# A decode layer's last microseconds on one core: output copies that no longer wait for each other, residual products issued ahead of the last matrix, and weight loads in fewer pieces

## The chip, the core and the metric

The kernel runs on one core of a Trainium2 chip. The metric is the device time of one execution in microseconds (us). The median of three runs of the kernel before is 190.62 us (190.58 to 190.89).

## What is computed

One token goes through attention with a cache of 16384 keys and values, then through a mixer and an MLP. The reference, cut to its core:

```python
def _A_ref(x, k_cache, v_cache, wq, wo):        # 32 query heads, 8 key heads, 128 wide
    q = (x @ wq) ...                            # one token, D = 512
    scores = einsum("bhqd,bhkd->bhqk", q, k) * (Dh ** -0.5)
    o = einsum("bhqk,bhkd->bhqd", softmax(scores), v)
    return o... @ wo
def _B_ref(x, w1, w2, w3, w4):
    h = _gelu(_layernorm(x) @ w1)
    hs = (four quarters of h, shifted along the sequence, zeros shifted in) @ w2
    x1 = x + hs
    return x1 + _gelu(_layernorm(x1) @ w3) @ w4   # F = 1792

h = x + _A_ref(_layernorm(x), ...)
return h + _B_ref(_layernorm(h), ...)
```

The sequence has length 1, so each shifted quarter holds only the zeros that were shifted in: hs is 0, x1 is x, and w1 and w2 are not needed.

## The kernel before, in words

Each engine has its own list of operations, written by hand in program order. A small class (`Program`, from L25) derives the waits: an operation names the tiles that it reads (`r`) and writes (`w`), and the PSUM banks that it touches (`bank`). Two engines that name the same bank wait for each other in program order, even if neither writes it. A list is issued in order, so an operation that waits holds everything behind it on its engine.

**Attention.** Four pairs of key heads are worked off one after another. Keys come in halves of 4 MB into `kb[0]` and `kb[1]`, values in 8 MB into `vb` (for the last pair in two pieces of 4 MB). DVE transposes the keys into `kt` (L583), PE multiplies them with the query (L600), ACT takes the exponentials (L621), and PE multiplies these with the values (L636). DVE gathers the pair's rows out of PSUM (L652 to L660) into `o_m`.

**Weights at the end.** The key buffers are used again: `wo` lies over `kb[0]`, `w3` and `w4` over `kb[1]`. All loads are issued on SP's queue by `load` (L434) in program order. `wo` is cut by `WO` (L329) into heads, `w3` by `W3` (L331) into chunks of 128 rows, and `w4` by `W4` (L332) into chunks m; each piece has a key of its own, `("r", 0, n)` for wo and `("r", 1, n)` for w3 and then w4. Each piece holds a stretch of every partition's row, so a piece of 12 heads moves 128 runs of 12 KB. SP waits until DVE has transposed the last keys of a buffer before it issues the loads that overwrite it.

**The tail.** DVE sums `o_m` into `o_f` (L696) and casts it to `o_b` (L698). PE multiplies it with wo: 32 matmuls, one for each head, in four column groups of 32 that run side by side (L702). DVE copies the result (L706), PE sums it over rows (L708), and `row_sums` (L479 to L495) makes the residual sum `hr`, its transpose `hT` and the moments of the layernorm. ACT adds the mean's negative into `hc` (L714), and PE multiplies `hc` with w3: 16 matmuls, four chunks by four column groups (L720). Meanwhile `variance` gives the scale, and DVE forms `xsum` (L724, L725), which is the residual plus its layernorm. ACT applies gelu in two halves (L729) and DVE transposes each half into `hcol` (L733). PE then multiplies `hcol` with w4: 14 chunks m by four column groups (L747). Between m = 6 and m = 7 it adds `xsum` by four fp32 products with the identity (L740); an fp32 matmul shows as two passes in the trace. All of it goes into one half of one PSUM bank, `n_ps` (bank "mn"). At the end ACT copies partitions 0 to 63 of it into `fin` (L752), DVE partitions 64 to 127 (L754), and SP sends two rows of `fin` to the output (L755).

Two operations without a function (L736 for DVE, L745 for PE) stand for branches that are never taken (L150, L314). They cut the two engines' last instructions into a block of their own.

Of the kernel before, what the change touches and what calls it, by code (L numbers as in the profile page):

```python
# [325 lines left out]
NCH = D // 128  # L326
FQ = FM // 4
NHC = FM // 128
WO = ((0, 12), (12, 24), (24, 30), (30, 32))  # L329
VP = 2  # L330
W3 = ((0, 2), (2, 3), (3, 4))  # L331
W4 = ((0, 5), (5, 10), (10, 13), (13, 14))  # L332
BLOCK = (0, 2, 1, 3)
PAIRS = HKV // 2
# [8 lines left out]
def bass_sequential_preLN__gqa_block_cached__mixer_s_mlp__decode_kernel(  # L343
# [13 lines left out]
    with ExitStack() as ctx:  # L357
# [18 lines left out]
        ident_f = sb("ident_f", [128, 128], FP32)  # L376
# [28 lines left out]
        o_f = sb("o_f", [128, 32], FP32)  # L405
        o_b = sb("o_b", [128, 32], BF16)
# [5 lines left out]
        xsum = sb("xsum", [128, 128], FP32)  # L412
# [3 lines left out]
        fin = sb("fin", [64, 256], BF16)  # L416
# [13 lines left out]
        m_ps, n_ps = mn_ps[:, 0:256], mn_ps[:, 256:512]  # L430


        def load(name, dst, src, key, by="SP", also=()):
            P.op(by, lambda e: e.dma_start(dst, src), w=[key, *also], dma=name)  # L434
# [24 lines left out]
        def dve(fn, r=(), w=(), bank=()):  # L459
            return P.op("DVE", fn, r, w, bank)  # L460

        def act(fn, r=(), w=(), bank=()):
            return P.op("ACT", fn, r, w, bank)
# [4 lines left out]
        def pe(fn, r=(), w=(), bank=(), also=()):  # L468

            return P.op("PE", fn, r, w, bank, also=also)  # L470

        def piece(cuts, m):
            return [lo <= m < hi for lo, hi in cuts].index(True)

        def copies(col, n):

            return col.to_broadcast([col.shape[0], n])
# [19 lines left out]
        def variance(i):  # L497

            s, S = st[i], ("st", i)

            dve(lambda e: e.scalar_tensor_tensor(s[:, 2:3], s[:, 0:1], s[:, 0:1], s[:, 1:2],
                                                 ALU.mult, ALU.add), r=[(S, 0)], w=[(S, 2)])
            dve(lambda e: e.tensor_scalar(s[:, 3:4], s[:, 2:3], 0.0, -1.0, ALU.min, ALU.mult),
                r=[(S, 2)], w=[(S, 3)])
            for n in range(1 + i):
                mul, add = (1.0 + EPS, EPS * EPS) if n else (1.0, EPS)
                dve(lambda e, n=n, mul=mul, add=add: e.tensor_scalar(s[:, 4 + n:5 + n], s[:, 3:4], mul, add,  # L507
                                                                     ALU.mult, ALU.add), r=[(S, 3)], w=[(S, 4 + n)])
            pool(lambda e: e.tensor_tensor(s[:, 6:7 + i], s[:, 4:5 + i], expo[:, 0:1 + i], ALU.pow),  # L509
                 r=["expo"] + [(S, 4 + n) for n in range(1 + i)], w=[(S, 6 + n) for n in range(1 + i)])  # L510
# [17 lines left out]
            r=["ident", "x4"], w=["quarter"])  # L528
        pe(lambda e: e.matmul(O_ps[0][:, 0:128], quarter[:, :, :].rearrange("p q u -> p (q u)"), x4[:, :],
                              start=True, stop=True), r=["quarter"], w=[("O", 0)], bank=[("O", 0)])  # L530
# [7 lines left out]
            r=["ident_f"], w=["row32"])  # L538
        dve(lambda e: e.tensor_reduce(maskdd[:, :], ident_f[:, :].rearrange("p (n d) -> p d n", d=4), AX.X, ALU.add),
            r=["ident_f"], w=["maskdd"])  # L540
# [6 lines left out]
        for z, m, key, mk in ((zo, rowgh, "zo", "rowgh"), (zd, maskgh, "zd", "maskgh")):  # L547
# [5 lines left out]
            r=["hT", (("st", 0), 0), (("st", 0), 6)] + [("v", x) for x in range(VP)], w=["xn"])  # L553
# [3 lines left out]
        for i, key in enumerate(keys):  # L557
            P.part("query", i)
            for k in range(NCH):
                pe(lambda e, k=k: e.matmul(row[:, bass.ds(P.b, 512)], copies(xn[:, k:k + 1], 128),  # L560
                                           wq_k[:, k, bass.ds(P.c, REP * DH)], start=(k == 0), stop=(k == NCH - 1)),
                   r=["xn"], also=[("v", x) for x in range(VP)], w=["n" if key == "mn" else key], bank=[key])
        P.part()
        for g in range(2):
            half = banks[64 * g:64 * g + 64, PAIRS * g:PAIRS * g + PAIRS, :].rearrange("p j c -> p (j c)")
            for b in range(2):
# [3 lines left out]
                    r=["n" if x == "mn" else x for x in keys[PAIRS * g:PAIRS * g + PAIRS]], w=["qcol"],  # L570
                    bank=keys[PAIRS * g:PAIRS * g + PAIRS])
# [112 lines left out]
        act(lambda e: e.activation(scr[0:1, 1:2], mean4[0:1, 0:1], ACTF.Gelu_apprx_tanh), r=["mean4"], w=["scr"])  # L684
        for n, (lo, hi) in enumerate(WO):
            load(f"wo{n}", wo_sb[:, lo * D:hi * D], A_wo.rearrange("(p r) c -> p (r c)", p=128)[:, lo * D:hi * D],
                 ("r", 0, n))
        w3_in = B_w3.rearrange("(p k) f -> p k f", p=128)
        for n, (lo, hi) in enumerate(W3):
            load(f"w3{n}", w3_sb[:, lo:hi, :], w3_in[:, lo:hi, :], ("r", 1, n))  # L690
        w4_in = B_w4.rearrange("(p m) c -> p m c", p=128)
        for n, (lo, hi) in enumerate(W4):
            load(f"w4{n}", w4_sb[:, lo:hi, :], w4_in[:, lo:hi, :], ("r", 1, len(W3) + n))


        dve(lambda e: e.tensor_reduce(o_f[:, :], o_m[:, :, :].rearrange("p d r -> p r d"), AX.X, ALU.add),  # L696
            r=["o_m"], w=["o_f"])
        dve(lambda e: e.tensor_copy(o_b[:, :], o_f[:, :]), r=["o_f", ("r", 0, 0)], w=["o_b"])  # L698

        for r_ in range(32):  # L700
            q = r_ % 4
            pe(lambda e, r_=r_, q=q: e.matmul(O_ps[0][32 * q:32 * q + 32, :], copies(o_b[:, r_:r_ + 1], 32),  # L702
                                              wo_sb[:, r_ * D:(r_ + 1) * D], start=(r_ < 4), stop=(r_ >= 28)),
               r=["o_b"] + [("r", 0, n) for n in (piece(WO, r_),) if n], w=[("O", 0)], bank=[("O", 0)])
        h_ps, hkey = banks[:, 6, :], "spare0"
        dve(lambda e: e.tensor_copy(osum[:, :], O_ps[0][:, :]), r=[("O", 0)], w=["osum"], bank=[("O", 0)])  # L706
        for q in range(4):
            pe(lambda e, q=q: e.matmul(h_ps[32 * q:32 * q + 32, 0:128], copies(row32[:, 0:1], 32),  # L708
                                       osum[:, q * 128:(q + 1) * 128], start=True, stop=True),
               r=["osum", "row32"], w=[hkey], bank=[hkey])  # L710
# [4 lines left out]
            r=["hT", (S, 0)] + [("r", 1, 0)], w=["hc"])  # L715


        for k in range(NCH):
            for q in range(4):
                pe(lambda e, k=k, q=q: e.matmul(s_ps[32 * q:32 * q + 32, 0, 0:FQ], hc[:, k, :],  # L720
                                                w3_sb[:, k, q * FQ:(q + 1) * FQ], start=(k == 0), stop=(k == NCH - 1)),
                   r=["hc"] + [("r", 1, n) for n in (piece(W3, k),) if n], w=[("s", 0)], bank=[("s", 0)])
        variance(1)
        dve(lambda e: e.tensor_scalar(xs[:, :], hr[:, :], s[:, 0:1], None, ALU.add), r=["hr", (S, 0)], w=["xs"])  # L724
        dve(lambda e: e.scalar_tensor_tensor(xsum[:, :], xs[:, :], s[:, 6:7], hr[:, :], ALU.mult, ALU.add),  # L725
            r=["hr", "xs", (S, 6)], w=["xsum"])
        for n in range(2):
# [6 lines left out]
                hcol[:, lo:hi, :].rearrange("p m u -> p (m u)"),  # L734
                hg[:, :].rearrange("p (i m) -> p m i", m=NHC)[:, lo:hi, :]), r=[("hg", n)], w=[("hcol", n)])
        dve(None)  # L736
        for m in range(NHC):
            if m == NHC // 2:
                for o in range(4):
                    pe(lambda e, o=o: e.matmul(  # L740
                        n_ps[32 * o:32 * o + 32, 0:128], ident_f[:, 32 * BLOCK[o]:32 * BLOCK[o] + 32], xsum[:, :],
                        start=False, stop=False, skip_group_check=True),
                       r=["ident_f", "xsum"], w=["n"], bank=["mn"])
            if m == W4[-2][0]:
                pe(None)  # L745
            for o in range(4):
                pe(lambda e, m=m, o=o: e.matmul(  # L747
                    n_ps[32 * o:32 * o + 32, 0:128], hcol[:, m, :], w4_sb[:, m, BLOCK[o] * 128:(BLOCK[o] + 1) * 128],
                    start=(m == 0), stop=(m == NHC - 1),
                    skip_group_check=True),  # L750
                   r=[("hcol", 2 * m // NHC), ("r", 1, len(W3) + piece(W4, m))], w=["n"], bank=["mn"])
        act(lambda e: e.activation(fin[:, 0:128], n_ps[0:64, 0:128], ACTF.Identity),  # L752
            r=["n"], w=[("fin", 0)], bank=["mn"])
        dve(lambda e: e.tensor_copy(fin[:, 128:256], n_ps[64:128, 0:128]), r=["n"], w=[("fin", 1)], bank=["mn"])  # L754
        P.op("SP", lambda e: e.dma_start(out[0, 0:1, :].rearrange("o (q j) -> (o q) j", q=2), fin[31:33, :]),  # L755
             r=[("fin", 0), ("fin", 1)], w=["out"], dma="out")
        P.op("SP", lambda e: e.nop(), r=["out"])
# [31 lines left out]
```

## Time and profile before

| | us |
|---|---|
| median of three runs | 190.62 (190.58 to 190.89) |
| the profiled execution's own time | 191.29 |
| its span, first to last instruction | 189.7 |
| PE busy / DVE busy / ACT busy | 116.1 / 115.4 / 9.3 |
| moved by DMA | 79.19 MB, mean 417 GB/s |

How to read it: the span is what the profile covers; 1.6 us of the profiled execution lie outside it. Busy shares are averages over the whole span. The chain of waits is followed back from the last instruction, at each step to what released it. PE is TensorE's matmuls, PEld its weight loads, DVE VectorE, ACT ScalarE, SP SyncE; a q behind a name (SPq, DVEq, PEldq) is an engine's sequencer. Matmuls are pipelined and their ends are modelled. A load's "us to landing" runs from its issue on SP to the last of its 16 engines' reports.

### The profile page before, as it was taken

To read this page: it belongs to the slowest core of one execution; us is meant where nothing else is said; L and a number is where in the kernel's file an instruction comes from. 1 tells how busy PE (TensorE), PEld (TensorE's weight loads), DVE (VectorE), ACT (ScalarE), POOL (GpSimd) and SP (SyncE) were. 2 spreads that over 40 slices of the span, in tenths; PEclk is the share of its full clock that TensorE was granted. 3 is DMA by queue.
4 is the path that set the end of the run, shared out by engine and by line. 5 is a ranking of instruction groups with operands and counts; after the bars stand their busy time and mean duration, and the time that the engine had idled before them with its cause. 6 is when DMAs were issued, how large, how long until landed. Compare 5 with 4: busy or idle time off the path is not lost.

```text
span 189.7 us, 2177 instructions
## 1 busy us (share of the span) xinstructions
PE 116.1 (61%) x701; PEld 45.8 (24%) x701; DVE 115.4 (61%) x140; ACT 9.3 (5%) x16; POOL 5.7 (3%) x10
## 2 busy tenths in 40 slices
PE   1009709997194498950842999606539996094544
PEld 1004203442031143320310343202213432041113
DVE  4900799995514998945047989460469896604151
ACT  3000000000200000002000000020000000500020
POOL 1900000000000000000000000000000000000010
PEclk9999985999858589995597599975975999759955
DMA  6999999999899999997999998999999999999992
GB/s 221 442 435 442 442 442 449 442 442 442 380 435 408 435 553 428 442 442 339 435 428 422 477 401 387 442 442 435 442 442 442 428 428 415 422 402 416 411 411 106
DMA packets 3613, 79.19 MB, mean 417 GB/s; under 512 B 410, under 2 KB 540, under 8 KB 1564
## 3 DMA queue, kind: packets, MB, share of 16 engines
q1 hardware_dynamic: 3604, 79.17, 97.5%
q8 instruction: 1, 0.02, 0.0%
q10 hardware_dynamic: 8, 0.00, 0.0%
HBM read 79.17 MB, written 0.00 MB: 417 GB/s over the span
## 4 chain that ended last, share of the span: by engine, by line
DMA 66%; DVE 15%; PE 14%; issue 3%; SPq 1%; ACT 0%; DVEq 0%
DMA kb<-in_A_k_cache_dram 46%; DMA kb<-in_B_w_dram 14%; DVE kt L583 13%; PE banks L600 8%; DMA vb<-in_A_wq_dram 7%; PE banks L560 4%; SPq L434 1%; DVE qcol L567 1%; PE banks L594 1%; PE banks L747 1%; DVE qb L574 0%; PE banks L740 0%; DVE xn L551 0%; DVE fin L754 0%; ACT fin L752 0%
## 5 line engine op out<-in xcount | busy, mean ns | idle before, releaser
L583 DVE STREAM_TRANSPOSE kt<-kb 128x2048 int32<-128x2048 int32 (+1 forms) x37 | 71.3, 1988 | 5.8 <-DMA kb<-in_A_k_cache_dram 4.2
L600 PE MATMUL banks<-kt,qn 128*128 x256 | 69.8, 422 | 0.2
L600 PEld LDWEIGHTS banks<-kt,qn 128*128 x256 | 26.6, 104 | 41.9 <-issue 25.1
L636 PE MATMUL banks<-vb,pt 128*32 128x512 bf16 x256 | 22.8, 534 | 2.8 <-POOLq L449 2.8
L652 DVE TENSOR_SCALAR od<-banks,rowc 128x128 f32<-128x128 f32 x4 | 1.4, 351 | 24.7 <-PE banks L636 24.7
L594 PE MATMUL banks<-qn 128*128 128x512 bf16 x8 | 3.9, 494 | 18.4 <-DVE kt L583 18.4
L560 PE MATMUL banks<-vb,xn 128*128 x32 | 8.4, 428 | 10.1 <-DVE xn L551 10.1
L625 DVE STREAM_TRANSPOSE pt<-p_sb 64x1024 bf16<-64x1024 bf16 x8 | 9.9, 1239 | 5.4 <-ACT p_sb L621 5.3
L636 PEld LDWEIGHTS banks<-vb,pt 128*32 128x32 bf16 x256 | 8.6, 130 | 15.2 <-issue 10.3
L621 ACT ACTIVATE p_sb<-banks,bias 128x1024 bf16<-128x1024 f32 x4 | 4.5, 1114 | 155.8 <-DVE nmh L617 155.8
L643 PE MATMUL banks<-acc,zd 128*32 128x1 f32 x8 | 1.1, 203 | 17.7 <-DVE pt L625 17.7
L610 DVE TENSOR_REDUCE mx<-banks 128x1 f32<-128x1024 f32 x4 | 4.9, 1224 | 8.1 <-PE banks L600 8.1
L567 DVE STREAM_TRANSPOSE qcol<-banks 64x1024 f32<-64x1024 f32 x4 | 4.8, 1226 | 6.4 <-PE banks L560 6.4
L560 PEld LDWEIGHTS banks<-vb,xn 128*128 128x128 bf16 x32 | 3.5, 108 | 14.6 <-issue 11.8
L509 POOL TENSOR_TENSOR st<-st,expo 128x1 f32<-128x1 f32 (+1 forms) x2 | 1.3, 630 | 176.1 <-DVE st L507 176.1
L613 PE MATMUL banks<-mxd,mean 128*128 128x128 f32 x8 | 2.0, 326 | 6.6 <-DVE mxd L611 6.6
L594 PEld LDWEIGHTS banks<-qn 128*128 128x128 bf16 x8 | 0.8, 100 | 20.8 <-issue 20.5
L658 PE MATMUL banks<-od,zo 128*32 128x128 f32 x8 | 1.6, 284 | 6.5 <-DVE od L655 6.5
L643 PEld LDWEIGHTS banks<-acc,zd 128*32 128x32 f32 x8 | 0.7, 140 | 18.4 <-DVE pt L625 18.4
L655 DVE SCALAR_TENSOR_TENSOR od<-banks,rowc,od 128x128 f32<-128x128 f32 x12 | 4.2, 351 | 0.4
L702 PE MATMUL banks<-kb,o_b 128*32 128x512 bf16 x32 | 2.7, 384 | 2.4 <-DMA kb<-in_A_wo_dram 1.3
L548 DVE COPY zo<-rowgh 128x32 f32<-128x32 f32 x1 | 3.6, 3627 | 0.0
(71 smaller groups left out, 42.4 us busy)
## 6 DMA issues: line engine op xcount, KB each, us to landing
kb<-in_A_k_cache_dram SPq DMA_DIRECT2D x8, 4096.0 KB, 29.7
vb<-in_A_v_cache_dram SPq DMA_DIRECT2D x2, 4096.0 KB, 29.6
vb<-in_A_wq_dram SPq DMA_DIRECT2D x1, 4096.0 KB, 12.6
kb<-in_A_wo_dram SPq DMA_DIRECT2D x2, 1536.0 KB, 25.4
kb<-in_B_w_dram SPq DMA_DIRECT2D x2, 640.0 KB, 25.4
kb<-in_B_w_dram SPq DMA_DIRECT2D x1, 896.0 KB, 22.4
kb<-in_B_w_dram SPq DMA_DIRECT2D x2, 448.0 KB, 23.4
kb<-in_A_wo_dram SPq DMA_DIRECT2D x1, 768.0 KB, 28.5
```

Source lines behind the costliest of these rows:

```text
L548: dve(lambda e, z=z, m=m: e.tensor_copy(z[:, :].rearrange("p (n d) -> p n d", d=4), m[:, :, :].rearrange("p g h -> p (g h)").unsqueeze(2). ...
L560: pe(lambda e, k=k: e.matmul(row[:, bass.ds(P.b, 512)], copies(xn[:, k:k + 1], 128), wq_k[:, k, bass.ds(P.c, REP * DH)], start=(k == 0), s ...
L567: dve(lambda e, g=g, b=b, half=half: e.transpose(qcol[64 * g:64 * g + 64, 2 * b:2 * b + 2, :, :].rearrange("p e m u -> p (e m u)"), half.r ...
L583: P.op("DVE", lambda e, view=view: e.transpose(view(kt), view(kb[y])), r=[("r", y, i) for i in range(RPARTS)], w=[("kt", t + i) for i in r ...
L594: pe(lambda e: e.matmul(row[:, bass.ds(P.y, 512)], copies(none, 128), copies(none, 512), start=True, stop=False, skip_group_check=True), r ...
L600: pe(lambda e, n=n: e.matmul(row[:, bass.ds(P.y, 512)], qn[:, n, bass.ds(P.q, 128)], key_piece(P.k, n), start=False, stop=(n == 3), skip_g ...
L610: dve(lambda e: e.tensor_reduce(mx[:, :], s_all, AX.X, ALU.max), r=[("s", 0), ("s", 1)], w=["mx"], **both)
L621: act(lambda e: e.activation(p_sb[:, :], s_all, ACTF.Exp, bias=bias[:, 0:1], scale=float(SCALE), accum_out=acc[:, :]), r=[("s", 0), ("s", ...
L625: dve(lambda e, g=g: e.transpose(pt[64 * g:64 * g + 64, :, :, g, :], p_sb[64 * g:64 * g + 64, :]), r=["p"], w=["pt"])
L636: pe(lambda e, l=l, ct=ct, ch=ch: e.matmul(O_ps[0][32 * ct:32 * ct + 32, :], pt[:, l, ch, :, :].rearrange("p g u -> p (g u)"), tiles[:, l ...
L655: dve(lambda e, block=block, c=c: e.scalar_tensor_tensor(od[:, :], block, rowc[:, c:c + 1], od[:, :], ALU.mult, ALU.add), r=[key, "rowc", ...
L702: pe(lambda e, r_=r_, q=q: e.matmul(O_ps[0][32 * q:32 * q + 32, :], copies(o_b[:, r_:r_ + 1], 32), wo_sb[:, r_ * D:(r_ + 1) * D], start=(r ...
```

## The change

It edits four things:

- the projection's 32 heads are loaded in pieces of 24, 6 and 2 instead of 12, 12, 6 and 2, and the third matrix's four chunks in pieces of 3 and 1 instead of 2, 1 and 1;
- the wait for the first projection piece goes from DVE's cast to PE's first matmul of the projection;
- the four products of `xsum` with the identity stand ahead of all of the last matrix's, and begin the accumulation in its place;
- DVE's output copy no longer names the bank, so that it waits for PE alone and not for ACT's copy.

```diff
-WO = ((0, 12), (12, 24), (24, 30), (30, 32))
+WO = ((0, 24), (24, 30), (30, 32))
 VP = 2
-W3 = ((0, 2), (2, 3), (3, 4))
+W3 = ((0, 3), (3, 4))
 W4 = ((0, 5), (5, 10), (10, 13), (13, 14))
...
-        dve(lambda e: e.tensor_copy(o_b[:, :], o_f[:, :]), r=["o_f", ("r", 0, 0)], w=["o_b"])
+        dve(lambda e: e.tensor_copy(o_b[:, :], o_f[:, :]), r=["o_f"], w=["o_b"])
...
-               r=["o_b"] + [("r", 0, n) for n in (piece(WO, r_),) if n], w=[("O", 0)], bank=[("O", 0)])
+               r=["o_b", ("r", 0, piece(WO, r_))], w=[("O", 0)], bank=[("O", 0)])
...
+        for o in range(4):
+            pe(lambda e, o=o: e.matmul(
+                n_ps[32 * o:32 * o + 32, 0:128], ident_f[:, 32 * BLOCK[o]:32 * BLOCK[o] + 32], xsum[:, :],
+                start=True, stop=False, skip_group_check=True),
+               r=["ident_f", "xsum"], w=["n"], bank=["mn"])
         for m in range(NHC):
-            if m == NHC // 2:
-                for o in range(4):
-                    pe(lambda e, o=o: e.matmul(
-                        n_ps[32 * o:32 * o + 32, 0:128], ident_f[:, 32 * BLOCK[o]:32 * BLOCK[o] + 32], xsum[:, :],
-                        start=False, stop=False, skip_group_check=True),
-                       r=["ident_f", "xsum"], w=["n"], bank=["mn"])
             if m == W4[-2][0]:
                 pe(None)
             for o in range(4):
                 pe(lambda e, m=m, o=o: e.matmul(
                     n_ps[32 * o:32 * o + 32, 0:128], hcol[:, m, :], w4_sb[:, m, BLOCK[o] * 128:(BLOCK[o] + 1) * 128],
-                    start=(m == 0), stop=(m == NHC - 1),
+                    start=False, stop=(m == NHC - 1),
                     skip_group_check=True),
...
         act(lambda e: e.activation(fin[:, 0:128], n_ps[0:64, 0:128], ACTF.Identity),
             r=["n"], w=[("fin", 0)], bank=["mn"])
-        dve(lambda e: e.tensor_copy(fin[:, 128:256], n_ps[64:128, 0:128]), r=["n"], w=[("fin", 1)], bank=["mn"])
+        dve(lambda e: e.tensor_copy(fin[:, 128:256], n_ps[64:128, 0:128]), r=["n"], w=[("fin", 1)])
```

## The prediction

> **What bounds the kernel now.** I read the page first, for the share of each resource.
>
> ```profile
> span 189.7 us, 2177 instructions
> ...
> q1 hardware_dynamic: 3604, 79.17, 97.5%
> q8 instruction: 1, 0.02, 0.0%
> ...
> DMA 66%; DVE 15%; PE 14%; issue 3%; SPq 1%; ACT 0%; DVEq 0%
> ```
>
> One queue of loads, q1, keeps the 16 DMA engines at work for 97.5% of the span, and two thirds of the chain that ended last is DMA. All four edits lie behind the last key load, so I read the end of the chain in order of time (columns: start, length, what).
>
> ```profile
> 158.70 0.43 SPq L434
> ...
> 160.12 25.99 DMA kb<-in_B_w_dram
> ...
> 186.16 0.41 PE banks L747 x7
> 186.56 0.43 PE banks L740 x6
> 186.99 0.77 PE banks L747 x22
> ...
> 187.78 0.28 ACT fin L752
> ...
> 188.09 0.02 DVEq L137
> ...
> 188.16 0.29 DVE fin L754
> ```
>
> The end has three pieces: a piece of the fourth matrix lands at 186.11; PE works without a pause to 187.76; then two copies run one behind the other, ACT from 187.78 to 188.06, DVE from 188.16 to 188.45. DVE reads PSUM only after ACT has finished, with 0.10 us of handover between them. But the chain follows one releaser only, so I asked whether the last load would have held PE anyway. The issues of the loads and the timeline of PE say so.
>
> ```profile
> L434 SPq DMA_DIRECT2D kb<-in_B_w_dram x7: 328/432/5841, 158.3 to 169.2; - x7
> ```
>
> ```profile
> kb<-in_B_w_dram SPq DMA_DIRECT2D x1, 128.0 KB, 18.2
> ```
>
> ```profile
> 185.05 0.73 PE L747 MATMUL banks<-kb,hcol 128*32 128x128 bf16 x20 [1.21 <-DVE hcol L733]
> ...
> 186.34 0.65 PE L740 MATMUL banks<-xsum,ident_f 128*32 128x128 f32 x8
> 186.77 0.97 PE L747 MATMUL banks<-kb,hcol 128*32 128x128 bf16 x28
> 188.52 0.33 SPq L755 DMA_DIRECT2D out_dram<-fin  x1
> ```
>
> ```profile
> L747 PE MATMUL banks<-kb,hcol x56: 286/314/315, 185.0 to 187.4; 128*32 128x128 bf16 x56
> ```
>
> The last piece (128 KB, for m = 13) was issued at 169.2 and landed 18.2 us later, at 187.4. Twenty matmuls, five groups of four that run side by side, take 0.73 us; one takes 0.31 (min, median and max are 286, 314 and 315 ns), so a new group starts every (0.73 - 0.31)/4 = 0.105 us. Seven groups from 186.77 would end at 186.77 + 6 x 0.105 + 0.31 = 187.71, and they ended at 187.74. So PE and the loads reach the last group within 0.03 us of each other, with the loads a hair later. The end is set by the load stream, and behind it by 188.52 - 187.74 = 0.78 us of copies and handovers.
>
> **The copies side by side.** The edit takes DVE's wait for ACT away: both now wait for the last matmul alone. What DVE needs to pick up a finished PE result is seen once before:
>
> ```profile
> 177.86 1.05 PE L702 MATMUL banks<-kb,o_b 128*32 128x512 bf16 x8 [1.07 <-DMA kb<-in_A_wo_dram]
> ...
> 178.95 0.69 DVE L706 COPY osum<-banks 128x512 f32<-128x512 f32 x1 [4.08 <-PE banks L702]
> ```
>
> It starts 0.04 us after PE's end (177.86 + 1.05 = 178.91), as fast as ACT's 0.05 (187.74 to 187.78). So DVE starts at about 187.78 instead of 188.16 and ends at 188.07 instead of 188.45; ACT ends at 188.06. The output's DMA, issued 0.07 us after DVE's end, moves from 188.52 to 188.15: **0.37 us**. No row of before has ACT and DVE read one PSUM bank at the same time, so this needs bounds: at best 0.38 (the whole difference of the starts); at worst the two reads take turns and only the 0.10 of handover goes, 0.09 to 0.10. Below nothing I see no way, since taking turns is what before does. I take 0.37, because the two copies read different partitions (0 to 63 and 64 to 127).
>
> [...]
>
> **The loads in fewer pieces.** The third matrix goes from pieces of 2, 1 and 1 chunks to 3 and 1, the projection from 12, 12, 6 and 2 heads to 24, 6 and 2. The bytes are the same; the runs per partition are longer: the projection's first 24 heads come in runs of 24 KB instead of 12 KB, three chunks in runs of 10.5 KB instead of 7 and 3.5. What a run's length is worth stands in the stretches of the stream (last columns: granted clock, DMA share, GB/s): 32 KB runs in the first, 12 KB in the second, mostly 7 and 3.5 KB in the third, 5 and 3 KB in the fourth.
>
> ```profile
> 159.00:165.00 6.00, 0.95 (x5) 0.30 (x2) 3.50 (x7) 2.69 (x4) 0.00 (x0) 0.88 1.00 431
> 168.50:174.50 6.00, 3.75 (x46) 1.38 (x38) 1.95 (x6) 0.00 (x0) 0.00 (x0) 0.84 1.00 425
> 179.40:182.40 3.00, 1.26 (x14) 0.80 (x18) 1.95 (x12) 0.40 (x1) 0.00 (x0) 0.71 1.03 413
> 182.40:185.40 3.00, 1.79 (x32) 0.62 (x28) 1.49 (x4) 0.85 (x2) 0.70 (x1) 0.50 1.00 402
> ```
>
> The engines are busy throughout, and the rate falls with the run's length: 431, 425, 413, 402. Between 12 KB (425) and 32 KB (431) 24 KB stands at about 429, so 3.15 MB take 7.33 us instead of 7.40: 0.07. Three chunks are 1.38 MB; at 413 they take 3.33 us, at 423 (a little under the 12 KB row) 3.25: 0.08. Together the stream ends **0.15 us** earlier. Bounds: 0 if the stretches differ for another reason than the runs, 0.24 if both merged pieces move at 431.
>
> What waits longer for merged pieces is hidden. The projection's matmuls first:
>
> ```profile
> 174.69 0.18 DVE L698 CAST o_b<-o_f 128x32 bf16<-128x32 f32 x1
> ...
> 174.93 0.83 PE L702 MATMUL banks<-kb,o_b 128*32 128x512 bf16 x12 [1.05 <-DVE o_b L698]
> ...
> 175.96 0.83 PE L702 MATMUL banks<-kb,o_b 128*32 128x512 bf16 x12 [0.20 <-DMA kb<-in_A_wo_dram]
> ```
>
> DVE's cast shows no wait for the first piece, so moving that wait from DVE to PE is worth nothing. But PE's first 12 matmuls now wait with the others for 24 heads, which land where the second piece does now (175.96) less 0.07. Twelve take 0.83 us, 0.22 per group of four behind the first, so 24 take 0.83 + 3 x 0.22 = 1.5 and end at 177.4. The next six wait for their load until 177.86 - 0.07 all the same: hidden with 0.4 us to spare. Everything from the copy at 178.95 on comes 0.07 us earlier with the projection's last piece. Then the third matrix:
>
> ```profile
> 181.51 0.16 DVE L495 COPY st<-banks 128x2 f32<-128x2 f32 x1 [0.37 <-PE banks L493]
> 181.70 0.40 ACT L714 ACTIVATE hc<-hT,st 128x128 bf16<-128x128 f32 x1 [16.75 <-DVE st L495]
> 182.15 1.68 PE L720 MATMUL banks<-kb,hc 128*32 128x448 bf16 x16 [0.69 <-ACT hc L714]
> ...
> 183.25 0.35 DVE L725 SCALAR_TENSOR_TENSOR xsum<-xs,st,hr 128x128 f32<-128x128 f32 x1 [0.70 <-POOL st L509]
> ```
>
> ```profile
> kb<-in_B_w_dram SPq DMA_DIRECT2D x1, 448.0 KB, 23.1
> ```
>
> ACT's hc now waits for three chunks, which land where the second piece does (158.70 + 23.1 = 181.8) less 0.15: 181.65. It starts at 181.70 now, so no later than before. SP issues two DMAs fewer, about 0.43 us each by the chain's row at 158.70, far ahead of their landings: worth nothing.
>
> **Residual's products first.** Four fp32 matmuls (eight passes, 0.65 us at this clock of 0.50) move from between m = 6 and m = 7 to ahead of m = 0. Their input ends at 183.25 + 0.35 = 183.60, PE is free from 182.15 + 1.68 = 183.83, and the first L747 starts at 185.05, so they end by about 184.5, hidden in 1.21 us of waiting. On the path they took 0.43 us of the chain. That is not gained: the last group waits for its load at 187.4 whatever precedes it. It gives PE 0.43 + 0.03 us of slack, so that the stream alone sets the end. Moving them back would cost about nothing, too: both the piece at 186.11 and the last one would move with the stream. I enter 0.
>
> **The sum.** 0.37 + 0.15 + 0 = 0.52 us. The profiled execution took 191.29 us (span 189.7, 1.6 outside it) and would take 190.77. The median of the runs is 190.62, so 0.67 under the profiled one; the same 0.52 off gives **190.10 us**.
>
> **The rivals.**
>
> *The two copies take turns* (0.12). For it: one bank, and no row shows the pair together. Against it: different partitions. Gain 0.09 + 0.15 = 0.24, so 190.38.
>
> *The loads get no shorter* (0.11): the stream's rate falls for another reason (other work at the end, other addresses), and merging changes nothing. For it: the four rates come from four different moments. Against it: they fall in the order of the run's length. Gain 0.37, so 190.25.
>
> *The code fetch runs into the last loads* (0.13), slower. One 16 KB packet of code, on a queue of its own, is fetched near the end, behind PE's branch at L314. The rows are the branch, the DMA engines in the microsecond from 186.3 (40 slices of 25 ns), and those from 187.3 (slices of 27.5 ns):
>
> ```profile
> L314 PEldq COMPARE_BRANCH  x1: 73/73/73, 186.3 to 186.3; - x1
> ```
>
> ```profile
> DMA  2240110300001011010101101000000000000000
> ...
> DMA packets 23, 0.02 MB, mean 22 GB/s; under 512 B 6, under 2 KB 21, under 8 KB 23
> ```
>
> ```profile
> DMA  0900000000000000000000000000000000000000
> ...
> q8 instruction: 1, 0.02, 5.3%
> ```
>
> The last packets of the loads trickle out, about one engine's worth, until 186.9, and the fetch starts at 187.34, taking 5.3% of 16 engines x 1.1 us = 0.93 us of one engine. If PE's branch starts it, 1.05 us lies between them. PE's sequencer runs ahead of its matmuls: it passed the branch at 186.3, while the 12 matmuls ahead of it began at 186.77. In the changed kernel the four fp32 matmuls no longer stand between m = 6 and the branch, so the sequencer can pass it before the piece at 186.11 lands, as early as about 185.5, where the last of the 20 matmuls before that wait starts (185.05 + 4 x 0.105). The fetch would start at about 186.55, while one engine still loads until 186.9 - 0.15 = 186.75. It decides from a branch before 186.75 - 1.05 = 185.7, and only if the fetch sits on that one engine; on any of the others the loads are over by then. Price: at most 0.93 us, the whole fetch ahead of the last packets: 190.62 - 0.52 + 0.93 = 191.03. Against it: one engine in 16, and nothing ties the fetch to the branch but the order in time.
>
> [...]
>
> **How the numbers follow.** The forecast has 0.64, the rivals 0.12, 0.11 and 0.13. About 0.2% (0.38 us) is what a measurement of this kernel can tell from no change. The forecast's own cases, 0.37 plus 0.05 to 0.24, lie beyond it (faster 0.64); turns (0.24) and loads no shorter (0.37) lie within it (same 0.23); the fetch is slower (0.13). The range: its low end takes both best bounds, 190.62 - 0.38 - 0.24 = 190.00, and 0.05 for the runs' spread; its high end takes turns without any gain of the loads, 190.62 - 0.09 = 190.53, and the same 0.05. Only the fetch is left out.
>
> **What would show it.** Right: in the chain's end ACT's and DVE's fin both start 0.05 us behind PE's last matmul, and the output's DMA 0.37 us after that; the last load lands 0.15 us earlier than at 187.4; L738 (L740 before) lies between 183.8 and 184.6; PE's last group waits for its DMA and nothing ahead of it. Wrong: DVE's fin at about twice its 0.29 us or still behind ACT; a q8 packet before 186.8 with a late last load; hc starting after 181.75; PE still busy when the last piece lands.

## The result, and the profile after

Over 20 runs of each the changed kernel takes 190.49 us in the median (190.10 to 191.35) and the kernel before 190.88 us (190.58 to 191.33). The ratio is 0.9983, with a 95% interval from 0.9977 to 0.9990: **0.32 us faster (0.19 to 0.44)**, where 0.52 was forecast. Between the forecast time, 190.10 us, and the measured one lie 0.39 us; 0.26 of them are the kernel before itself, whose three runs gave 190.62 as the start of the forecast.

The first view is the page and the end of the chain of waits of the changed kernel (start, length, what).

```profile
span 188.8 us, 2175 instructions
...
159.79 26.82 DMA kb<-in_B_w_dram
...
186.65 0.65 PE banks L746 x12
...
187.32 0.29 DVE fin L753
```

The chain is the forecast one but for one piece: a load, PE's last groups, one copy; ACT's copy and its handover are gone from it. The load that it names is the piece before the last, for m = 10 to 12, which landed at 186.61 (159.79 + 26.82). The last piece landed at 186.89, 0.07 us before the last group started, so PE's last wait was for the piece ahead of it, and not for the last one as forecast. In the timeline of the same execution the copies start at the same moment, 0.05 us behind PE's end (186.65 + 0.62), the output's DMA follows 0.37 us after their start, and the residual's products (L738) run while PE has nothing else to do.

```profile
175.63 3.53 PE L702 MATMUL banks<-kb,o_b 128*32 128x512 bf16 x32 [2.76 <-DMA kb<-in_A_wo_dram]
...
179.22 0.69 DVE L706 COPY osum<-banks 128x512 f32<-128x512 f32 x1 [5.34 <-PE banks L702]
...
183.81 0.66 PE L738 MATMUL banks<-xsum,ident_f 128*32 128x128 f32 x8
...
184.98 1.39 PE L746 MATMUL banks<-kb,hcol 128*32 128x128 bf16 x40 [0.52 <-DVE hcol L733]
...
186.65 0.62 PE L746 MATMUL banks<-kb,hcol 128*32 128x128 bf16 x16 [0.28 <-DMA kb<-in_B_w_dram]
187.32 0.27 ACT L751 ACTIVATE fin<-banks 64x128 bf16<-64x128 f32 x1 [2.64 <-PE banks L746]
187.32 0.29 DVE L753 CAST fin<-banks 64x128 bf16<-64x128 f32 x1 [1.93 <-PE banks L746]
187.69 0.33 SPq L754 DMA_DIRECT2D out_dram<-fin  x1
```

One line is not as forecast. The projection's matmuls (L702) run without a pause from 175.63 to 179.16, and DVE's copy behind them starts at 179.22, later than the 178.95 of before. The stretches say why (the last three columns are granted clock, DMA share, GB/s):

```profile
176.00:178.00 2.00, 2.00 (x24) 0.93 (x20) 0.00 (x0) 0.00 (x0) 0.00 (x0) 0.50 1.09 438
178.00:180.00 2.00, 1.20 (x16) 0.22 (x10) 0.69 (x1) 0.00 (x0) 0.00 (x0) 0.76 1.00 419
```

The clock is granted by half (0.50) while PE works off its 24 heads. In the profile of before these matmuls ran at a clock of 1.00:

```profile
176.00:178.00 2.00, 0.93 (x16) 0.30 (x18) 0.00 (x0) 0.00 (x0) 0.00 (x0) 1.00 1.05 415
```

(The half clock shows without the merged loads too: e1, below, has 0.50 in the same stretch.)

The two profiles must not be subtracted as they stand: 189.7 against 188.8 overstates the change. The profiled execution of before (191.29 us) lies at the upper end of its 20 runs, and in it one of the 16 DMA engines reported the last load 0.45 us behind the other 15 (187.39 against 186.94; after: 186.89 against 186.85). Each run also lists its span, and means over runs serve better: in 33 runs of before (those beside the first four experiments) the span is 189.30 us with **1.54 us outside it**; in the 20 runs of the changed kernel it is 188.86 with **1.70 outside**. The span gave 0.44 us, near the forecast; behind it 0.16 us were lost again. The two make 0.28 us, within the interval above.

### The profile page after: what moved, and what is told of

The parts are those of the page before. It is cut to its first block, busy times and chain, and to the rows that moved or that the text cites. A ratio compares the mean times of both kernels' runs of the same rounds, so it can differ in the third digit from the quotient of the medians.

```text
span 188.8 us, 2175 instructions
## 1 busy us (share of the span) xinstructions
PE 116.5 (62%) x701; PEld 45.5 (24%) x701; DVE 115.4 (61%) x140; ACT 9.3 (5%) x16; POOL 5.7 (3%) x10
## 4 chain that ended last, share of the span: by engine, by line
DMA 66%; DVE 17%; PE 9%; issue 6%; SPq 1%; DVEq 0%
DMA kb<-in_A_k_cache_dram 45%; DVE kt L583 15%; DMA kb<-in_B_w_dram 14%; DMA vb<-in_A_wq_dram 7%; PE banks L560 5%; PE banks L600 4%; SPq L434 1%; DVE qcol L567 1%; DVE qb L574 0%; PE banks L746 0%; PE banks L594 0%; DVE xn L551 0%; DVE fin L753 0%; SPq L137 0%; DVEq L137 0%
## 5 line engine op out<-in xcount | busy, mean ns | idle before, releaser
L636 PE MATMUL banks<-vb,pt 128*32 128x512 bf16 x256 | 21.3, 505 | 2.9 <-POOLq L449 2.9
L560 PE MATMUL banks<-vb,xn 128*128 x32 | 9.4, 467 | 9.8 <-DVE xn L551 9.8
L636 PEld LDWEIGHTS banks<-vb,pt 128*32 128x32 bf16 x256 | 8.0, 123 | 14.3 <-issue 8.5
L702 PE MATMUL banks<-kb,o_b 128*32 128x512 bf16 x32 | 3.5, 621 | 2.8 <-DMA kb<-in_A_wo_dram 2.8
L706 DVE COPY osum<-banks 128x512 f32<-128x512 f32 x1 | 0.7, 692 | 5.3 <-PE banks L702 5.3
```

Source lines behind the costliest of these rows:

```text
L636: pe(lambda e, l=l, ct=ct, ch=ch: e.matmul(O_ps[0][32 * ct:32 * ct + 32, :], pt[:, l, ch, :, :].rearrange("p g u -> p (g u)"), tiles[:, l ...
```

## The experiments

The theories, by the letters that the expectations use. *A*: each part gives what was forecast. *B*: the copies lose part of their gain, by turns on the bank or behind the span. *C*: the merged loads are to blame, because they make PE's projection one late burst. *D*: the span shrinks as forecast, but PE's code fetch, started by its branch at L314, keeps the execution from ending sooner. *E* comes with the last experiments: an early branch has a gain of its own.

Every ratio is against the kernel before on the same chip; "outside" is the time less the span, as a mean over runs. e9 has 5 runs and e11 has 4, the other experiments 11 each.

| kernel | ratio (95%) | span | outside (highest) |
|---|---|---|---|
| before | 1 | 189.30 to 189.41 | 1.51 to 1.54 (1.69) |
| the changed kernel, 20 runs | 0.9983 (0.9977 to 0.9990) | 188.86 | 1.70 (2.07) |
| e1 copies alone | 0.9977 (0.9968 to 0.9986) | 188.90 | 1.55 (1.72) |
| e2 loads alone | 1.0007 (0.9998 to 1.0016) | 189.37 | 1.59 (1.65) |
| e3 products alone | 1.0003 (0.9994 to 1.0012) | 189.42 | 1.49 (1.60) |
| e4 all, again | 0.9990 (0.9978 to 1.0001) | 188.85 | 1.83 (2.43) |
| e5 all, projection in 4 pieces | 0.9983 (0.9974 to 0.9992) | 188.92 | 1.60 (1.77) |
| e6 all, third matrix in 3 pieces | 0.9984 (0.9975 to 0.9993) | 188.94 | 1.66 (2.05) |
| e7 copies and products | 0.9980 (0.9971 to 0.9989) | 188.96 | 1.57 (1.74) |
| e8 copies and loads | 0.9981 (0.9972 to 0.9990) | 188.90 | 1.57 (1.64) |
| e9 all, branch at m = 13 | 1.0150 (1.0134 to 1.0165) | 188.80 | 4.50 (5.06) |
| e10 all, branch at m = 5 | 0.9974 (0.9965 to 0.9983) | 188.86 | 1.52 (1.67) |
| e11 copies, branch at m = 13 | 1.0145 (1.0130 to 1.0161) | 188.98 | 4.74 (4.98) |
| e12 as e5, branch at m = 5 | 0.9977 (0.9968 to 0.9986) | 188.90 | 1.52 (1.66) |
| e13 before, branch at m = 5 | 0.9997 (0.9988 to 1.0006) | 189.35 | 1.52 (1.64) |
| e14 all, branch at m = 0 | 0.9978 (0.9969 to 0.9987) | 188.87 | 1.60 (1.67) |

### The parts, one at a time

```diff
-... tensor_copy(fin[:, 128:256], n_ps[64:128, 0:128]), r=["n"], w=[("fin", 1)], bank=["mn"])
+... tensor_copy(fin[:, 128:256], n_ps[64:128, 0:128]), r=["n"], w=[("fin", 1)])
```

> The kernel before with one edit: DVE's output copy no longer waits for ACT's. Theory A (the copies give what was forecast, the shortfall lies elsewhere): both copies start together, the output's DMA 0.37 us sooner behind PE's last matmul, time 0.3 to 0.4 us under before. Theory B (the copies' gain is partly lost behind the span or by turns on the bank): 0.1 to 0.2 us under before, and DVE's copy longer than 0.29 us if it is the bank.

Measured: 0.44 us under before (0.27 to 0.61), span 0.40 shorter, outside as before. The timeline of e1 has both copies start together, at their old lengths:

```profile
187.35 0.27 ACT L752 ACTIVATE fin<-banks 64x128 bf16<-64x128 f32 x1 [3.02 <-PE banks L747]
187.36 0.29 DVE L754 CAST fin<-banks 64x128 bf16<-64x128 f32 x1 [2.29 <-PE banks L747]
```

A holds for the copies, and B falls: nobody takes turns.

This kernel also speaks to C, since its projection is still loaded in four pieces. Its matmuls and the stretch that they lie in (the last three columns as above):

```profile
175.29 3.42 PE L702 MATMUL banks<-kb,o_b 128*32 128x512 bf16 x32 [1.05 <-DVE o_b L698]
```

```profile
176.00:178.00 2.00, 2.00 (x24) 0.75 (x18) 0.00 (x0) 0.00 (x0) 0.00 (x0) 0.50 1.04 414
```

All 32 matmuls run without a pause here too, those from 176 to 178 us at half the clock (0.50), 3.42 us against 3.53 in the changed kernel. So the late burst by which C explains the loss does not need the merged loads.

```diff
-WO = ((0, 12), (12, 24), (24, 30), (30, 32))
-W3 = ((0, 2), (2, 3), (3, 4))
+WO = ((0, 24), (24, 30), (30, 32))
+W3 = ((0, 3), (3, 4))
```

(with the wait moved from DVE's cast to PE's first matmul, as in the change)

> The kernel before with the merged loads alone (24, 6, 2 heads; 3, 1 chunks; the wait for the first piece moved to PE's first matmul). Theory A, as forecast: the stream's end 0.15 us earlier, time 0.1 to 0.2 us under before. Theory C (the merged loads give nothing, or PE's 24 matmuls, waiting longer, cost what the shorter stream gives): within 0.1 us of before or over it.

Measured: no gain, rather a loss (0.13 us over, -0.04 to +0.31). Yet the stream did get shorter. From the last values' landing to the last load's landing it takes 18.86 us in before, 18.84 in e1 and e3, and 18.69 in e2 (18.70 in the changed kernel and e8, 18.72 in e4). With one merged piece it is 18.77 (projection, e6) and 18.79 (third matrix, e5): 0.15 us in all, half from each, as forecast. Kernels with neither merge, e7 and e11, have 18.84 and 18.83; e13 alone stands apart with 19.00. The spans of e2's runs are spread: four at 189.1, 0.2 under before, the others from 189.3 up to 189.8. The timeline of e2's profiled execution, with a span of 189.4, has this end:

```profile
185.02 1.24 PE L747 MATMUL banks<-kb,hcol 128*32 128x128 bf16 x28 [1.20 <-DVE hcol L733]
185.85 0.14 PEld L747 LDWEIGHTS banks<-kb,hcol 128*32 128x32 bf16 x8 [0.38 <-DMA kb<-in_B_w_dram]
...
186.47 1.01 PE L747 MATMUL banks<-kb,hcol 128*32 128x128 bf16 x28
187.53 0.27 ACT L752 ACTIVATE fin<-banks 64x128 bf16<-64x128 f32 x1 [2.81 <-PE banks L747]
```

It does not show a late PE. PE reaches the last matrix at 185.02 (185.05 in before), a piece of the loads still holds its weights until 185.85, and its last group starts at 187.15, 0.04 us behind the last landing at 187.11. C's figure, no gain, is met; its mechanism is not seen, and the slower runs have no trace.

Counted from the last values' landing to the span's end, the traced executions follow the forecast's terms: 21.15 us in before, 21.16 in e3 (products first), 21.01 in e2 (loads), 20.78 in e1 (copies), 20.65 in the changed kernel. What lies ahead of that landing differs between the executions (it falls between 168.00 and 168.53 us), and the edited loads stand behind these values in SP's queue, so the edits give no reason for it.

```diff
+        for o in range(4):
+            pe(lambda e, o=o: e.matmul(
+                n_ps[32 * o:32 * o + 32, 0:128], ident_f[:, 32 * BLOCK[o]:32 * BLOCK[o] + 32], xsum[:, :],
+                start=True, stop=False, skip_group_check=True),
...
         for m in range(NHC):
-            if m == NHC // 2:
-                for o in range(4):
...
```

> The kernel before with the residual's four products ahead of the last matrix alone. Both theories: within 0.1 us of before, because PE's last group waits for its load whatever precedes it. If PE rather than the load sets the end in most runs, up to 0.4 us under before.

Measured: 0.06 us over before (-0.11 to +0.23). Alone the move gives nothing that can be told from 0, as forecast.

The changed kernel again, beside its parts:

> The changed kernel itself again, beside its parts on one chip. Theory A: its gain is the sum of the three parts, about 0.5 us. Theory C: about that of the copies alone, 0.3 to 0.4 us.

Measured: 0.19 us under before (0.42 under to 0.02 over). The span, 188.85, is the forecast's; the time outside is 1.83 in the mean, and in two of 11 runs 2.36 and 2.43. No part alone has that; the highest of e1 to e3 is 1.72. The gain, 0.19 us, lies under the figures of both theories, though its interval reaches C's 0.3 to 0.4. So something behind the span, which none of the three parts alone brings out, takes back a part of what the span gives.

### Which parts bring it out

> The changed kernel with the projection's loads in four pieces again (12, 12, 6, 2 heads). Theory C (PE's burst of 24 matmuls, waiting for 24 heads, is what eats the gain): back to the copies' gain, 0.4 us under before, and the time outside the span back at 1.5 us. Theory D (the span shrinks as forecast, but something behind the span's end, PE's late code fetch, takes it back when the residual's products stand first): no change from the changed kernel, 0.2 to 0.3 us under before, time outside the span 1.7 to 1.8 us.

> The changed kernel with the third matrix's loads in three pieces again (2, 1, 1 chunks). If one merged piece is to blame and it is this one: 0.4 us under before. Else as the changed kernel, 0.2 to 0.3 us under before.

> Before with the copies side by side and the residual's products first, loads as before. Theory C (the merged loads are to blame): 0.4 us under before, as with the copies alone, time outside the span 1.5 us. Theory D (the order of PE's end is to blame, through the code fetch): 0.1 to 0.3 us under before, time outside the span 1.7 us or more.

> Before with the copies side by side and the merged loads, residual's products in the middle as before. Theory C: 0.2 us under before or less. Theory D: 0.4 to 0.5 us under before, time outside the span 1.5 us.

The edits are those of the first four, put together as the names say (e5 and e6 take one of the two `WO` and `W3` lines back). Measured: 0.31 to 0.38 us under before in all four; their intervals overlap, so the times do not say which piece is to blame. Neither theory is met alone: e7, for which D expected 1.7 us or more outside, has 1.57, and e8, for which C expected 0.2 us or less, is 0.36 us under before. The runs' spreads say a little. With the products in the middle (e8) the time outside stays at 1.64 or less. With the products first and 24 heads in one piece (e6, e4, the changed kernel) it reaches 2.05 to 2.43. The longest spans tell nothing: 189.4 in e8, 189.3 in the changed kernel, 189.2 in e5. The profiled execution of e6, with 1.93 us outside, shows both sides. Two of its stretches, and its timeline:

```profile
178.00:180.00 2.00, 1.22 (x12) 0.18 (x4) 0.69 (x1) 0.00 (x0) 0.00 (x0) 0.50 1.00 409
180.00:182.00 2.00, 1.23 (x10) 0.71 (x10) 0.92 (x5) 0.00 (x0) 0.00 (x0) 0.50 1.04 413
```

```profile
185.60 1.69 PE L746 MATMUL banks<-kb,hcol 128*32 128x128 bf16 x56 [0.64 <-DVE hcol L733]
187.34 0.27 ACT L751 ACTIVATE fin<-banks 64x128 bf16<-64x128 f32 x1 [2.05 <-PE banks L746]
```

The clock stays at 0.50 here, so PE reaches the last matrix at 185.60 (184.98 in the changed kernel's profile, where the clock came back to 1.00 in between). The projection ended at nearly the same time in both, 179.22 and 179.16. With the products out of the way its 56 matmuls run through without a pause and still end with the loads: the copies start at 187.34. But the branch and the fetch come late as well. The branch's row, and the DMA engines in the 2 us from 187.2 (40 slices of 50 ns):

```profile
L314 PEldq COMPARE_BRANCH  x1: 73/73/73, 186.1 to 186.1; - x1
```

```profile
DMA  0900000000000000000000000000000000000000
...
q8 instruction: 1, 0.02, 3.5%
```

The fetch starts at 187.26 and takes 3.5% of 16 engines x 2 us = 1.1 us, to 188.37. The same rows of the changed kernel, from 186.7:

```profile
L314 PEldq COMPARE_BRANCH  x1: 73/73/73, 185.7 to 185.7; - x1
```

```profile
DMA  0900000000000000000000000000000000000000
...
q8 instruction: 1, 0.02, 3.0%
```

There the branch stands at 185.7 and the fetch from 186.78 to 187.72, and only 1.53 us lie outside that execution's span.

### Moving the branch

In the changed kernel (e9) and in the one with the copies alone (e11) the branch goes from ahead of m = 10 to ahead of m = 13:

```diff
-            if m == W4[-2][0]:
+            if m == W4[-1][0]:
                 pe(None)
```

> The changed kernel with PE's never-taken branch moved from ahead of m = 10 to ahead of m = 13. Theory D (the branch starts the code fetch, and the execution can't end sooner than about 2.2 to 2.4 us behind the fetch's end): branch and fetch about 0.9 us later, the span as in the changed kernel (188.85), time outside the span 2.2 us or more, 0.3 us or more over before. Theory C (PE's late burst alone, no matter where the branch stands): no change from the changed kernel, 1.7 us outside the span.

> The copies side by side alone, with PE's branch ahead of m = 13. Theory D: the same floor shows without merged loads and without the moved products: span 188.9, time outside the span 2.2 us or more, over before. Theory C: as the copies alone, 1.5 us outside the span, 0.4 us under before.

Measured: 2.9 us (e9) and 2.8 us (e11) **over** before, though the spans, 188.80 and 188.98, are those of the kernels without the move. The rows of e9 (engines from 188.3) and of e11 (engines from 190.9):

```profile
L314 PEldq COMPARE_BRANCH  x1: 73/73/73, 186.8 to 186.8; - x1
```

```profile
DMA  9000000000000000000000000000000000000000
...
q8 instruction: 1, 0.02, 3.6%
```

```profile
L314 PEldq COMPARE_BRANCH  x1: 73/73/73, 186.9 to 186.9; - x1
```

```profile
DMA  9000000000000000000000000000000000000000
...
q8 instruction: 1, 0.02, 3.7%
```

In e11 the fetch starts at 190.93, behind the span's end at 189.05. In both the end follows the fetch and not the span: 2.43 us (e9) and 1.87 us (e11) lie between the fetch's end and the execution's. D's direction holds, also without merged loads and moved products (e11), and the size is ten times that of the loss to be explained. So a late branch can hold the end back. Whether it does so in the changed kernel, where it stands three chunks earlier, is for the next move to show.

The other way, to ahead of m = 5, in the changed kernel (e10) and in e5 (e12):

```diff
-            if m == W4[-2][0]:
+            if m == W4[1][0]:
                 pe(None)
```

> The changed kernel with PE's never-taken branch ahead of m = 5. Theory D: branch and fetch 0.5 to 0.9 us sooner, time outside the span 1.5 us in all runs, 0.45 us under before, unless the fetch now meets the last loads (the prediction's third rival), which shows as a span longer by 0.3 to 0.9 us. Theory C: 1.7 us outside the span, as the changed kernel.

> A candidate to beat both: the changed kernel with the projection's loads in four pieces again and PE's branch ahead of m = 5. Theory D: span 188.9, 1.5 us outside it, 0.4 to 0.5 us under before, with no run over 190.7. Theory C: as the same kernel without the branch's move, 190.5.

Measured: e10 is 0.50 us under before (0.32 to 0.67) with a span of 188.86 and 1.52 us outside, at most 1.67. **That is about the forecast's 0.52 us, from the changed kernel with its branch 20 matmuls earlier.** By the ratios alone it can't be told from the changed kernel, since the intervals overlap (0.32 to 0.67 and 0.19 to 0.44). The time outside parts them: 1.52 with a highest of 1.67 against 1.70 with 2.07, and 1.83 with 2.43 in e4. By C the branch would have left it at 1.7; C falls as the sole cause. e12 is 0.44 under (0.27 to 0.61) and can't be told from it. The branch of e10:

```profile
L314 PEldq COMPARE_BRANCH  x1: 73/73/73, 185.2 to 185.2; - x1
```

What the profiled executions have in common (us; one execution of each kernel):

| | branch | fetch | span's end | time | outside | time less fetch's end |
|---|---|---|---|---|---|---|
| before | 186.3 | 187.34 to 188.27 | 189.68 | 191.29 | 1.61 | 3.02 |
| changed | 185.7 | 186.78 to 187.72 | 188.84 | 190.37 | 1.53 | 2.65 |
| e1 | 185.8 | 187.05 to 188.05 | 188.88 | 190.28 | 1.40 | 2.23 |
| e12 | 185.3 | 186.55 to 187.95 | 188.86 | 190.36 | 1.50 | 2.41 |
| e5 | 185.7 | 186.88 to 188.24 | 188.80 | 190.43 | 1.63 | 2.19 |
| e4 | 185.6 | 187.17 to 188.09 | 188.73 | 190.53 | 1.80 | 2.44 |
| e6 | 186.1 | 187.26 to 188.37 | 188.88 | 190.81 | 1.93 | 2.44 |
| e7 | 186.0 | 187.27 to 188.58 | 189.07 | 190.84 | 1.77 | 2.26 |
| e9 | 186.8 | 188.34 to 189.49 | 188.90 | 191.92 | 3.02 | 2.43 |
| e11 | 186.9 | 190.93 to 192.11 | 189.05 | 193.98 | 4.93 | 1.87 |
| e10 | 185.2 | 186.30 to 187.28 | 188.89 | 190.46 | 1.57 | 3.18 |
| e2 | 186.0 | 187.21 to 188.29 | 189.43 | 190.90 | 1.47 | 2.61 |
| e3 | 186.0 | 187.49 to 188.42 | 189.42 | 190.87 | 1.45 | 2.45 |
| e8 | 185.6 | 186.74 to 187.71 | 188.70 | 190.30 | 1.60 | 2.59 |
| e13, below | 185.4 | 186.67 to 187.75 | 189.57 | 190.97 | 1.40 | 3.22 |
| e14, below | 183.4 | 185.98 to 187.08 | 188.66 | 190.27 | 1.61 | 3.19 |

Where 0.64 us or less lies between the fetch's end and the span's end, 1.6 us or more lie outside; where 0.8 us or more does, 1.4 to 1.6. The time is never less than 1.87 us behind the fetch's end, and but for e11 not less than 2.19. It is a floor with some play, not a sharp line.

The control is the same move in the kernel before:

```diff
-            if m == W4[-2][0]:
+            if m == W4[1][0]:
                 pe(None)
```

> Control: the kernel before with only PE's branch moved from ahead of m = 10 to ahead of m = 5. Theory D (the fetch costs only where the span ends too soon behind it): the fetch starts sooner, but the time outside the span is 1.5 us already, so within 0.1 us of before. Theory E (an early branch gains 0.1 to 0.3 us for any kernel, and the moved branch did not give the lost gain back but brought one of its own): 0.1 to 0.3 us under before.

Measured: 0.9997 (0.9988 to 1.0006), so E falls: before ends late enough behind its fetch, and one that starts 0.67 us earlier (186.67 against 187.34) gives it nothing.

And the branch in the changed kernel further ahead still, behind the residual's products:

```diff
-            if m == W4[-2][0]:
+            if m == 0:
                 pe(None)
```

> The changed kernel with PE's branch ahead of m = 0, behind the residual's products. It prices the prediction's third rival: the code fetch of 0.9 to 1.4 us then starts at about 185, with loads still queued on every DMA engine. If fetch and loads share an engine as the rival says, the last load lands 0.3 to 0.9 us later and the span grows to 189.2 to 189.7; if not, span 188.85 and time outside it 1.5 us, as with the branch ahead of m = 5.

Measured: 0.42 us under before (0.25 to 0.59), span 188.87: the last load is not late (18.71 us behind the last values' landing). The branch and the engines from 185.9:

```profile
L314 PEldq COMPARE_BRANCH  x1: 73/73/73, 183.4 to 183.4; - x1
```

```profile
DMA  9975520000000000000000000000000000000000
...
q8 instruction: 1, 0.02, 3.4%
```

The branch is 1.8 us earlier than in e10, the fetch only 0.3 us: it starts at 185.98, 2.6 us behind its branch, where the loads are running out, and not at about 185 as expected. Its first 0.7 us lie beside the last loads, which land by 186.71, and delay none of them. The rival's collision does not show even here.

## Why the prediction was off

- **The copies, 0.37 us: right.** e1's span is 0.40 shorter, both copies keep their lengths (0.27 and 0.29 us), and they start 0.05 us behind PE. The two copies do not take turns. That this is so because they read different partitions (0 to 63 and 64 to 127) was the author's estimate; no run has both copies on the same ones.
- **The loads, 0.15 us: right as a length of the stream, not found in the means over runs.** The stream takes 18.68 to 18.72 us in every kernel with both merges, against 18.83 to 18.86 without (19.00 in e13). From the last values' landing to the span's end the changed kernel's profile is 0.50 us shorter than that of before and 0.13 shorter than e1's. But the mean span of e4 is only 0.05 under that of e1, and that of e2 is 0.07 over before; why the means do not show the 0.15 stays open. One step was wrong without deciding the end: "hidden with 0.4 us to spare" took the rate of 12 matmuls at a clock of 1.00. At 0.50 (0.53 as the mean of 175.60 to 179.20) the projection runs from 175.63 to 179.16 and ends 0.25 us later than in before, where 0.07 sooner was forecast. PE reached the last matrix at 184.98 all the same. From 176 to 178 us the clock was 1.00 in the execution of before and 0.50 in others, with merged loads (the changed kernel) and without (e1); what sets it was not shown.
- **The products first, 0: right.** e3 can't be told from before. "Moving them back would cost about nothing" holds too: e8 is the changed kernel with the products in the middle, and it is 0.36 us under before with 1.57 us outside.
- **The step that failed** is in the sum: "The profiled execution took 191.29 us (span 189.7, 1.6 outside it) and would take 190.77." It took the 1.6 us as a constant. They are not: as a mean over runs they grew from 1.54 us to 1.70 in the changed kernel's 20 runs and to 1.83 in e4's 11, so 0.16 to 0.29 us of the forecast were lost again behind the span. The traced executions have long times outside where PE's code fetch ends late, and the earlier branch of e10, with nothing else changed, brings the 1.52 us back. Of the changed kernel's own longer runs one is traced, e4's with 1.80 us outside, and there the fetch ends only 0.64 us ahead of the span's end; the runs with 2.36 and 2.43 us have no trace. The rest of the miss is the mean span, 0.44 us shorter where 0.52 was forecast. The shorter span alone does not do it: e1's is 0.40 shorter, and it has 1.55 us outside.
- **The rival of the code fetch** had the right part and the wrong place. It tied the fetch to the branch, which e9 to e13 confirm, but looked for its price in the loads. That a fetch ahead of the last packets would delay them was the author's estimate, and the runs do not show it: e14's fetch, whose branch stood at 183.4, was seen only at 185.98, and no load was late (the last one landed 18.71 us behind the last values' landing, against 18.70 in the changed kernel). The price came behind the span, where the prediction expected no change.

Open: why the time from branch to fetch differs, from 1.0 to 1.6 us in most executions to 2.6 in e14 and 4.0 in e11; and what makes the fetch late in some runs of the changed kernel. The traces show two ways: a late branch (186.1 in e6, at half the clock; 186.0 in e7, without merged loads) and a long way from branch to fetch (185.6 to 187.17 in e4).

## What to carry to other kernels

Compare time less span between the runs of two kernels as well as the spans: a kernel that ends sooner can be held by something that was free until then, here the code fetch behind PE's branch (in e9 it ended at 189.49, and 3.02 us lay outside the span). When an edit shortens the end, look for the code fetch in the DMA queues and ask how far in front of the last instruction it ends; if a branch of your own starts it, move that branch with the edit. And price a burst of matmuls at the half clock too: from 176 to 178 us, in the projection, the clock was 1.00 in one execution (before) and 0.50 in others, with merged loads (the changed kernel) and without (e1).

## What was not expected of the hardware

The execution's end lay 1.9 to 2.4 us behind the end of the code fetch in all traced executions whose fetch ended less than 0.95 us ahead of the span's end or behind it, also where the last instruction was long done (e11: fetch to 192.11, span's end 189.05, time 193.98). With the branch three chunks of the last matrix later, from m = 10 to m = 13, the time was 2.8 us (e11) and 2.9 us (e9) over before. In the profile of before one DMA engine reported each load 0.42 to 0.46 us behind the other 15; in the changed kernel's profile the last two reports lie 0.04 us apart. Which it is differs between executions and hides edits of 0.1 us in a comparison of single profiles.
